# Expert blocks behind run-time branches: order of the two versions, row lists, weight halves, and a version for a last short block

## The chip, the cores and the metric

One core of one Trainium2 chip runs the whole kernel. The metric is the device time of one execution in microseconds (us). The engines are PE (matrix multiplication, with PEld for its weight loads), DVE (vector), ACT (scalar functions), POOL (general purpose; here it issues gathers and scatters) and SP (here it issues plain transfers). Each engine has a sequencer of its own that fetches instructions, waits for semaphores and takes branches; in the profile its rows carry a q (PEldq, DVEq, POOLq).

## The reference, cut to what matters

Three layers in a row, all in float32: local and global attention, a dense layer of width 2048, and a routed layer with 8 experts. The part that the change touches is the last:

```python
skip_score = x @ w_skip
do_compute = skip_score > 0
out = x.copy()
xc = x[do_compute]
logits = xc @ w_gate
e_idx = np.argmax(logits, axis=1)
...
for e in range(E):
    mask = e_idx == e
    if not mask.any():
        continue
    h = np.maximum(xc[mask] @ w1[e], 0.0)
    y[mask] = gate_w[mask, None] * (h @ w2[e])
out[do_compute] = xc + y
```

Which rows go to which expert is known only at run time. For the inputs that are timed, worked out from the reference, 1389 of the 2304 rows are computed: 1116 by expert 3, 241 by expert 0, 32 by expert 5, and none by the other five.

## The kernel before, in words

Attention and the dense layer come first and are not touched. While the dense layer runs, each row tile is routed (`route`, L458): its rows' numbers go to a table in memory, one stretch for each expert, and `choose_first` (L566) picks the expert with most rows so far. Its weights are loaded, split into a high and a low part on ACT and DVE (`split`, L631), and its first 256 rows are computed in code without branches (L804 to L820, the **first block**).

`choose_order` (L581) then sorts what is left: 1116 - 256 = 860 rows of the first expert (called expert 0 from here on, by its place in the order), 241 of expert 1, 32 of expert 2, none of experts 3 to 7. DVE does this with some twenty operations on a single partition, and writes the counts and the start of each row list to `regs` and `nxt`. Each engine loads the 8 counts into registers (L821) and from there on branches on them by itself.

A **block** is `(k, t)`: expert k, its t-th 256 rows. Each block exists in two versions (`products`, L824). The wide one does up to 256 rows: 8 x 12 matmuls to the hidden layer (`mm1`), 8 transposes for the next block's rows, 2 x 8 x 3 matmuls back (`mm2`). The few-row one does up to 128 with the operands exchanged: 24 matmuls of 512 columns (`mm1_few`), 8 transposes of the hidden layer, 24 matmuls back, and 8 transposes for the next block. With these counts the path is (0,0) wide, (0,1) wide, (0,2) wide, (0,3) few (92 rows), (1,0) wide, (2,0) few, and the end.

How the code lies in memory, and so what a branch skips:

- In `block` (L875) the wide version comes first, and the few-row version behind it as `Else`; a wide block ends with a jump past the few-row code.
- In `expert` (L894) the first block of an expert is there twice, with and without loading the next expert's weights (the test on the next count, L896), one behind the other.
- `others` (L888) holds the further blocks of the expert, each inside the test of the one before (L890); an expert that is done jumps past all blocks that it doesn't use (five for expert 0 behind (0,3), five for expert 1, three for expert 2).
- The next expert is inside the test of its count (L904). The end of the kernel lies behind all experts and behind a second copy of them (L909, used when the first expert has nothing left).

Where such paths meet again, every engine brings its semaphores to the same counts: the engine that comes along the shorter path adds what is missing, and first waits until its own work has reached its count. For POOL's semaphores of transfers that means a wait for the landing of its transfers.

What a block does around its matmuls: at its head DVE copies the row list (`cid`), POOL loads the list of the next block (`load_ids`, L877), and DVE and POOL finish the second half of the **block before** (`finish_rows(1)`, `send_rows(1)`, L881: scale, add, scatter to the output). Then the version's own code: POOL gathers the next block's rows (`load_rows`, two gathers of 128 rows), and in an expert's first block SP loads the next expert's weights, chunks 0 and 1 at the head and 2 to 7 behind the gathers; a POOL memset ahead of each group holds SP back until the buffer is free (`prefetch`, L797). The last `finish_rows(1)` and `send_rows(1)` stand behind all branches (L915).

Of the kernel before, what the change touches and what calls it, by code (L numbers as in the profile page):

```python
# [7 lines left out]
F32 = mybir.dt.float32  # L8
# [6 lines left out]
ALU = mybir.AluOpType  # L15
AX = mybir.AxisListType
ET = mybir.EngineType
# [11 lines left out]
NF = FF // 128  # L29
# [18 lines left out]
def tile_kernel(ctx, tc, q, k, v, w_in, w_out, wsg, w1, w2,  # L48
# [532 lines left out]
    def choose_order():  # L581
        cnt = counts()
        nc.vector.scalar_tensor_tensor(out=key, in0=cnt, scalar=8.0, in1=sev[0:1, :], op0=ALU.mult, op1=ALU.add)
        nc.vector.scalar_tensor_tensor(out=key, in0=ohs, scalar=65536.0, in1=key, op0=ALU.mult, op1=ALU.add)
        nc.vector.max(out=top, in_=key)
        nc.vector.tensor_copy(out=ki[:, 0:8], in_=top)
        nc.vector.tensor_scalar(out=regs[:, 8:16], in0=ki[:, 0:8], scalar1=7, scalar2=7, op0=ALU.bitwise_and,
                                op1=ALU.bitwise_xor)
        nc.vector.tensor_scalar(out=ki[:, 8:16], in0=ki[:, 0:8], scalar1=3, scalar2=4095,
                                op0=ALU.arith_shift_right, op1=ALU.bitwise_and)  # L590
        nc.vector.tensor_copy(out=cf, in_=ki[:, 8:16])
        nc.vector.tensor_tensor(out=cf[:, 0:1], in0=cf[:, 0:1], in1=s0, op=ALU.subtract)
# [5 lines left out]
        n1 = mp.tile([1, NE, NBM], F32, name="n1")  # L598
        n2 = mp.tile([1, NE, NBM], F32, name="n2")
        n3 = mp.tile([1, 8], F32, name="n3")  # L600
# [12 lines left out]

    def routing_step(u):
        if rt:
# [208 lines left out]
    def products(k, many, pre):  # L824
        q = k % 2
        todo = [(1 - q, f, raws[f // 2]) for f in range(NF)] if pre else []

        def splits(n=1):
            for _ in range(n):
                if todo:  # L830
                    split(*todo.pop(0))

        if many:
            nc.vector.tensor_copy(out=cyg_, in_=nyg_)
            for f in range(NEF):
                mm1(q, f)
                if f == 1:
                    load_rows()
                    if pre:
                        prefetch(k + 1, range(4 if k == 0 else 2, 8))  # L840
                if f >= (0 if k == 0 else 5):
                    splits()
            nc.vector.tensor_copy(out=pid, in_=cid[:, :, 0:2])
            for s_ in range(2):
                transpose_rows(s_)
            for s_ in range(2):
                for f in range(NEF):
                    mm2(q, s_, s_, f)
                    if f % 2 == 1:
                        splits()  # L850
                if s_ == 0:
                    finish_rows(0)
                    send_rows(0)
        else:
            nc.vector.tensor_copy(out=cyg_[:, 1], in_=nyg_[:, 0])
            load_rows()
            if pre:
                prefetch(k + 1, range(4 if k == 0 else 2, 8))
            mm1_few(q, 0)
            splits(1 if k == 0 else 0)  # L860
# [4 lines left out]
            splits()  # L865
            for f in range(NEF):
                mm2(q, 0, 1, f)
                if f == 1:
                    transpose_few(1)
                if f in (2, 3):  # L870
                    transpose_rows(f - 2)
                splits(2 if f % 2 == 0 else 1)
        splits(NF)

    def block(k, t, pre):  # L875
        nc.vector.tensor_copy(out=cid, in_=nid)
        load_ids(nc.values_load(nxt[0:1, k * NBM + t:k * NBM + t + 1], engines=[ET.Pool], min_val=0,  # L877
                                max_val=NE * CAP))
        if pre and k > 0:
            prefetch(k + 1, range(2))  # L880
        finish_rows(1)  # L881
        send_rows(1)
        with tc.If(cnts[k] > BLK * t + 128) as wide:
            products(k, True, pre)
        with wide.Else():
            products(k, False, pre)

    def others(k, t):  # L888
        if t < NBLK[k]:
            with tc.If(cnts[k] > BLK * t):  # L890
                block(k, t, False)
                others(k, t + 1)

    def expert(k):  # L894
        if k + 1 < NE:
            with tc.If(cnts[k + 1] > 0) as more:  # L896
                block(k, 0, True)
            with more.Else():
                block(k, 0, False)
        else:  # L900
            block(k, 0, False)
        others(k, 1)
        if k + 1 < NE:
            with tc.If(cnts[k + 1] > 0):  # L904
                expert(k + 1)

    with tc.If(cnts[0] > 0) as some:
        expert(0)
    with some.Else():  # L909
        with tc.If(cnts[1] > 0):  # L910
            prefetch(1, range(4, 8))
            for f in range(NF):
                split(1, f, raws[f // 2])
            expert(1)
    finish_rows(1)  # L915
    send_rows(1)


# [102 lines left out]
```

## Time and profile before

| what | us |
|---|---|
| median of 3 runs | 719.22 (717.91 to 720.38) |
| the profiled execution | 719.69 |
| its span, first to last instruction | 717.6 |
| PE busy in the span | 678.9 (95%) |
| mean granted PE clock | 0.984 |

The profiled execution is 0.47 above the median; its span leaves out 2.1 us around the first and last instruction. On the page, PE's row of busy tenths reads 9 or nearly in all but the first and the last slices of the span, and the last two slices read 4 and 3. The chain of work that ended last is PE for 71%, transfers for 8%, and "issue" for 6%: time in which an engine waited for nothing that the profile shows.

### The profile page before, as it was taken

To read this page: it belongs to the slowest core of one execution; us is meant where nothing else is said; L and a number is where in the kernel's file an instruction comes from. 1 tells how busy PE (TensorE), PEld (TensorE's weight loads), DVE (VectorE), ACT (ScalarE), POOL (GpSimd) and SP (SyncE) were. 2 spreads that over 40 slices of the span, in tenths; PEclk is the share of its full clock that TensorE was granted. 3 is DMA by queue.
4 is the path that set the end of the run, shared out by engine and by line. 5 is a ranking of instruction groups with operands and counts; after the bars stand their busy time and mean duration, and the time that the engine had idled before them with its cause. 6 is when DMAs were issued, how large, how long until landed. Compare 5 with 4: busy or idle time off the path is not lost.

```text
span 717.6 us, 11768 instructions
## 1 busy us (share of the span) xinstructions
PE 678.9 (95%) x4081; PEld 562.0 (78%) x4081; DVE 411.9 (57%) x1419; ACT 382.7 (53%) x904; POOL 80.7 (11%) x134
## 2 busy tenths in 40 slices
PE   6999999999999999999999999999999899999843
PEld 4777777778888777788777888898889799988632
DVE  6899999978998333334433254435666483223711
ACT  4888888967997443344433354436663162112501
POOL 2111111100000001000010000020002322222020
PEclk9999999999999999999999999999999999999967
DMA  9656566335540300003000033213101441205520
GB/s 301 187 169 183 169 169 209 117 103 172 158 138 0 118 0 1 1 1 117 1 1 1 1 117 118 59 31 102 47 2 60 157 170 58 60 33 136 195 48 15
DMA packets 28242, 66.83 MB, mean 93 GB/s; under 512 B 3755, under 2 KB 12589, under 8 KB 27108
## 3 DMA queue, kind: packets, MB, share of 16 engines
q1 hardware_dynamic: 25092, 58.41, 25.1%
q0 software_dynamic: 3040, 7.10, 3.6%
q8 instruction: 51, 0.84, 0.6%
q14 instruction: 59, 0.48, 0.3%
HBM read 53.38 MB, written 12.43 MB: 92 GB/s over the span
## 4 chain that ended last, share of the span: by engine, by line
PE 71%; DMA 8%; issue 6%; DVE 5%; ACT 1%; POOL 1%; POOLq 0%; DVEq 0%
PE y L534 26%; PE h L158 26%; DMA nyg<-ys,nid 6%; PE e L664 5%; PE z L699 3%; PE o L305 3%; PE t L290 2%; PE s L252 2%; DMA out_dram<-ob,pid 2%; PE r L465 1%; DVE P_a L261 1%; ACT P_a L268 1%; DVE P_a L284 1%; PE r L469 1%; DMA nid<-table 1%
## 5 line engine op out<-in xcount | busy, mean ns | idle before, releaser
L534 PE MATMUL y<-wout,gh 128*128 128x512 f32 x544 | 139.9, 396 | 0.1
L158 PE MATMUL h<-xh,winH 128*128 128x512 f32 (+2 forms) x320 | 118.2, 369 | 0.0
L534 PEld LDWEIGHTS y<-wout,gh 128*128 128x128 f32 x544 | 99.0, 188 | 20.4 <-issue 1.2
L158 PE MATMUL h<-xh,winL 128*128 128x512 f32 (+2 forms) x320 | 114.6, 358 | 0.0
L158 PE MATMUL h<-xl,winH 128*128 128x512 f32 (+2 forms) x320 | 114.4, 357 | 0.0
L517 DVE SCALAR_TENSOR_TENSOR tb<-tb,h 128x512 f32<-128x512 f32 (+2 forms) x80 | 48.5, 607 | 105.4 <-ACT tb L514 104.8
L513 ACT ACTIVATE tb<-h,misc 128x512 f32<-128x512 f32 (+2 forms) x80 | 49.6, 620 | 78.9 <-PE h L158 66.3
L534 PE MATMUL y<-wout,gl 128*128 128x512 f32 x272 | 74.9, 390 | 0.0
L521 DVE TENSOR_TENSOR gl<-tb,gh 128x512 fp32r<-128x512 f32 (+2 forms) x80 | 48.9, 611 | 41.9 <-ACT gh L518 41.6
L518 ACT ACTIVATE gh<-tb 128x512 fp32r<-128x512 f32 (+2 forms) x80 | 45.4, 567 | 45.0 <-DVE tb L517 44.4
L158 PEld LDWEIGHTS h<-xh,winH 128*128 128x128 f32 x320 | 60.2, 188 | 10.6 <-issue 2.5
L158 PEld LDWEIGHTS h<-xh,winL 128*128 128x128 f32 x320 | 60.2, 188 | 7.8
L158 PEld LDWEIGHTS h<-xl,winH 128*128 128x128 f32 x320 | 60.3, 189 | 7.4
L268 ACT ACTIVATE P_a<-P_a,st 128x160 f32<-128x160 f32 x128 | 53.8, 423 | 15.3 <-DVE st L261 14.4
L500 POOL DMA_INDIRECT table<-ids,slot x17 | 17.3, 1020 | 387.5 <-DVE slot L498 274.1
L534 PEld LDWEIGHTS y<-wout,gl 128*128 128x128 f32 x272 | 51.1, 188 | 11.0
L699 PE MATMUL z<-WA,h 128*128 128x512 f32 x240 | 57.9, 394 | 0.0
L305 PE MATMUL o<-PT,V 128*64 128x160 f32 x512 | 48.9, 311 | 2.6 <-issue 1.4
L699 PEld LDWEIGHTS z<-WA,h 128*128 128x128 f32 x240 | 44.2, 188 | 8.7
L664 PE MATMUL e<-yTH,WA 128*128 128x256 f32 x256 | 48.7, 286 | 0.1
L252 PE MATMUL s<-K,Q 128*128 128x160 f32 x256 | 46.3, 305 | 1.5 <-DVE st L261 1.3
L514 ACT ACTIVATE tb<-tb 128x512 f32<-128x512 f32 (+2 forms) x80 | 45.5, 568 | 2.5
(200 smaller groups left out, 1104.9 us busy)
## 6 DMA issues: line engine op xcount, KB each, us to landing
xr<-in_w_dram SPq DMA_DIRECT2D x24, 512.0 KB, 6.5
V<-in_v_dram SPq DMA_DIRECT2D x8, 1024.0 KB, 5.3
K<-in_k_dram SPq DMA_DIRECT2D x7, 800.0 KB, 5.3
raw<-in_w_in_dram SPq DMA_DIRECT2D x10, 512.0 KB, 6.3
sp<-in_w_out_dram SPq DMA_DIRECT2D x10, 512.0 KB, 4.5
ys<-xT SPq DMA_DIRECT2D x15, 256.0 KB, 3.0
out_dram<-xT SPq DMA_DIRECT2D x15, 256.0 KB, 4.6
Q<-in_q_dram SPq DMA_DIRECT2D x14, 256.0 KB, 6.6
```

Source lines behind the costliest of these rows:

```text
L158: nc.tensor.matmul(hp, lhsT=lw, rhs=rx[:, 0:n], start=(c == 0 and k == 0), stop=(c == 3 and k == 2))
L252: nc.tensor.matmul(s_ps[s % 2][:, a, 0:W], lhsT=Q_b[n % 2][:, i, j, :, :, a].rearrange("p h c -> p (h c)"), rhs=K_b[n % 2][:, i, W * j + 9 ...
L268: nc.scalar.activation(out=px(s, a), in_=px(s, a), func=AF.Exp, bias=st[:, a:a + 1], scale=-1.0, accum_out=st[:, 2 + a:3 + a])
L305: nc.tensor.matmul(o[64 * h:64 * h + 64, 0:W], lhsT=V[:, j, t, i * 128 + h * 64:i * 128 + h * 64 + 64], rhs=PT[:, t, h, :], start=(t == 0) ...
L513: nc.scalar.activation(out=t, in_=hp, func=AF.Relu, bias=half, scale=0.5)
L514: nc.scalar.activation(out=t, in_=t, func=AF.Square)
L517: nc.vector.scalar_tensor_tensor(out=t, in0=t, scalar=1.0, in1=hp, op0=ALU.min, op1=ALU.max)
L518: nc.scalar.activation(out=a, in_=t, func=AF.Copy)
L521: nc.vector.tensor_tensor(out=b_, in0=t, in1=a.bitcast(F32), op=ALU.subtract)
L534: nc.tensor.matmul(y_ps[q], lhsT=(gL if lows else gH)[:, s], rhs=wo(hl, f), start=(f == 0 and hl == 0 and not lows), stop=(f == NF - 1 and ...
L664: nc.tensor.matmul(hp, lhsT=lw, rhs=ry[:, c], start=(n == 0), stop=(n == 11))
L699: nc.tensor.matmul(z_ps[z], lhsT=lh[:, d], rhs=rw, start=(f == 0 and k == 0), stop=(f == NEF - 1 and k == 2))
```

## The change

1. `choose_order` computes, for each block, where the list of the block after next begins (`fr` holds the next ones, `nxt` becomes those one further), and `last[k]`: zero when expert k has at most 128 rows and no expert follows. The 8 values go to `regs[24:32]`, and every engine loads them as a second set of registers (`more`).
2. Row lists are a block further ahead: `next_ids` at the **end** of a block copies `nid` to `cid` and loads the list for the block after next; a block's gathers come at its very start. `finish_rows(1)` and `send_rows(1)` move from the next block's head to the end of the block itself, before its branch.
3. Weights come in two halves: `prefetch(k + 2, range(4))` behind the splits of block (k, 0), and `prefetch(k + 1, range(4, 8))` at the start of block (k, 0). An expert's first block always has the splits of the next expert's weights; they are no longer there in two copies.
4. The few-row version comes first in the code, the wide one behind it as `Else`, and the test for the expert's next block is inside the wide version. Block (1,0) has the wide version alone.
5. Experts 2 to 7 begin with a test of `more[k]`; where it is zero, `last_few` does the one short block with no gathers, no row lists and no transposes for a next block, and with its own finish and send.

```diff
+        last = sc[:, 56:64]
+        nc.vector.tensor_scalar(out=last, in0=cf, scalar1=-128.0, scalar2=0.0, op0=ALU.add, op1=ALU.max)
+        nc.vector.tensor_tensor(out=last[:, 0:7], in0=last[:, 0:7], in1=cf[:, 1:8], op=ALU.max)
+        nc.vector.tensor_copy(out=regs[:, 24:32], in_=last)
...
+        nc.vector.memset(o, float(NE * CAP))
         nc.vector.tensor_scalar(out=n3[:, 0:1], in0=cf[:, 0:1], scalar1=0.0, scalar2=None, op0=ALU.is_gt)
...
-        nc.vector.tensor_tensor(out=n1, in0=n1, in1=n2, op=ALU.mult)
-        nc.vector.tensor_tensor(out=nxt.rearrange("p (k t) -> p k t", k=NE), in0=n1, in1=bk1, op=ALU.add)
+        nc.vector.tensor_tensor(out=n2, in0=n1, in1=n2, op=ALU.mult)
+        nc.vector.tensor_tensor(out=fr[:, 0:NE, 0:NBM], in0=n2, in1=bk1, op=ALU.add)
...
+        nc.vector.tensor_tensor(out=nxt.rearrange("p (k t) -> p k t", k=NE), in0=n2, in1=fk1, op=ALU.add)
...
+    def next_ids(addr):
+        nc.vector.tensor_copy(out=cid, in_=nid)
+        load_ids(addr)
...
-        if q == 0:
-            finish_rows(0)
-            send_rows(0)
+        if q == 1:
+            next_ids(nc.values_load(regs[0:1, 17:18], engines=[ET.Pool], min_val=0, max_val=NE * CAP))
+        finish_rows(q)
+        send_rows(q)
     _, cnts = nc.values_load_multi_w_load_instructions(regs[0:1, 0:NE], min_val=0, max_val=TOK)
+    _, more = nc.values_load_multi_w_load_instructions(regs[0:1, 24:24 + NE], min_val=0, max_val=TOK)
...
+    def products(k, t, many):
         q = k % 2
+        pre = t == 0 and k + 1 < NE
...
         if many:
             nc.vector.tensor_copy(out=cyg_, in_=nyg_)
+            load_rows()
+            if pre:
+                prefetch(k + 1, range(4, 8))
             for f in range(NEF):
                 mm1(q, f)
-                if f == 1:
-                    load_rows()
-                    if pre:
-                        prefetch(k + 1, range(4 if k == 0 else 2, 8))
-                if f >= (0 if k == 0 else 5):
-                    splits()
+                splits()
...
-                if s_ == 0:
-                    finish_rows(0)
-                    send_rows(0)
+                if s_ == 1:
+                    next_ids(after(k, t))
+                finish_rows(s_)
+                send_rows(s_)
         else:
...
+            next_ids(after(k, t))
+            finish_rows(1)
+            send_rows(1)
         splits(NF)
+        if pre and k + 2 < NE:
+            prefetch(k + 2, range(4))
+
+    def last_few(k):
+        q = k % 2
+        nc.vector.tensor_copy(out=cyg_[:, 1], in_=nyg_[:, 0])
+        mm1_few(q, 0)
+        mm1_few(q, 1, range(2))
+        transpose_few(0)
+        mm1_few(q, 1, range(2, 4))
+        nc.vector.tensor_copy(out=pid[:, 1], in_=cid[:, 0, 0:2])
+        for f in range(NEF):
+            mm2(q, 0, 1, f)
+            if f == 1:
+                transpose_few(1)
         finish_rows(1)
         send_rows(1)
...
+    def wide(k, t):
+        products(k, t, True)
+        if t + 1 < NBLK[k]:
+            with tc.If(cnts[k] > BLK * (t + 1)):
+                block(k, t + 1)
+
+    def block(k, t):
+        if (k, t) == (1, 0):
+            wide(k, t)
+            return
+        with tc.If(cnts[k] <= BLK * t + 128) as few:
+            products(k, t, False)
+        with few.Else():
+            wide(k, t)
+
+    def following(k):
+        block(k, 0)
         if k + 1 < NE:
             with tc.If(cnts[k + 1] > 0):
                 expert(k + 1)
+
+    def expert(k):
+        if k < 2:
+            following(k)
+            return
+        with tc.If(more[k] == 0) as end:
+            last_few(k)
+        with end.Else():
+            following(k)
...
-    finish_rows(1)
-    send_rows(1)
```

## Rows read from the trace of the kernel before

**Rows 1.** The page: the span, and one of the queues that bring code.

```profile
span 717.6 us, 11768 instructions
...
q14 instruction: 59, 0.48, 0.3%
```

**Rows 2.** Time line of PE, 565 to 718: start, length, what, and idle time before it.

```profile
569.01 0.66 PE L653 MATMUL p<-ident,nyg 128*128 128x128 f32 x4 [1.06 <-DMA nyg<-ys,nid]
...
641.03 0.39 PE L679 MATMUL e<-WA,yTH 128*128 128x512 f32 x1
...
654.89 0.36 PE L664 MATMUL e<-yTH,WB 128*128 128x256 f32 x1 [0.94 <-DVE ob L704]
...
691.47 0.77 PE L679 MATMUL e<-WA,yTH 128*128 128x512 f32 x1 [13.03 <-issue]
...
704.17 1.75 PE L699 MATMUL z<-WA,h 128*128 128x512 f32 x7
```

**Rows 3.** PE's sequencer between blocks (1,0) and (2,0): branches, ns, start.

```profile
L883 PEldq COMPARE_BRANCH  x1: 3757/3757/3757, 674.2 to 674.2; - x1
...
L890 PEldq COMPARE_BRANCH  x1: 5057/5057/5057, 678.0 to 678.0; - x1
...
L896 PEldq COMPARE_BRANCH  x1: 4629/4629/4629, 683.4 to 683.4; - x1
...
L883 PEldq COMPARE_BRANCH  x1: 3177/3177/3177, 688.1 to 688.1; - x1
```

**Rows 4.** Windows: length, busy time of PE, PEld, DVE, ACT, POOL, then PE's granted clock.

```profile
680.80:691.40 10.60, 0.00 (x0) 0.00 (x0) 1.18 (x2) 0.00 (x0) 3.93 (x4) 0.50 0.33 77
691.40:694.50 3.10, 3.03 (x7) 2.48 (x8) 0.00 (x0) 0.00 (x0) 0.00 (x0) 0.50 0.03 8
```

**Rows 5.** Behind the last matmul: PE's branches, DVE's last operation, the last send.

```profile
L904 PEldq COMPARE_BRANCH  x1: 4993/4993/4993, 706.5 to 706.5; - x1
...
L904 PEldq COMPARE_BRANCH  x1: 4604/4604/4604, 711.7 to 711.7; - x1
...
712.57 0.75 DVE L704 SCALAR_TENSOR_TENSOR ob<-z,pid,cyg 128x512 f32<-128x512 f32 x1 [7.99 <-PEq L904]
...
713.61 1.02 POOL L708 DMA_INDIRECT out_dram<-ob,pid  x1 [25.54 <-DVE ob L704]
```

**Rows 6.** PE's sequencer at two other branches: past the few-row version; out of expert (0).

```profile
L883 PEldq COMPARE_BRANCH  x1: 193/193/193, 613.7 to 613.7; - x1
...
L890 PEldq COMPARE_BRANCH  x1: 3315/3315/3315, 650.5 to 650.5; - x1
```

**Rows 7.** The first block: register load of the counts (PE), one small DVE operation.

```profile
L821 PEldq TENSOR_LOAD <-regs x1: 780/780/780, 569.1 to 569.1; - x1
...
L604 DVE TENSOR_TENSOR regs<-n,sc 1x1 int32<-1x1 f32 x1 | 0.1, 147 | 0.0
```

**Rows 8.** DVE's sequencer at a branch past unused blocks, and its first step behind it, twice.

```profile
L890 DVEq COMPARE_BRANCH  x2: 47/55/63, 651.9 to 652.8; - x2
L890 DVEq EVENT_SEMAPHORE  x1: 21/21/21, 652.7 to 652.7; - x1
...
L890 DVEq COMPARE_BRANCH  x1: 62/62/62, 675.6 to 675.6; - x1
L890 DVEq EVENT_SEMAPHORE  x1: 21/21/21, 679.2 to 679.2; - x1
```

**Rows 9.** POOL at an expert's end: waits for transfers, counts; time behind a far branch.

```profile
L890 POOLq EVENT_SEMAPHORE  x5: 17/43/3889, 644.9 to 649.1; - x5
L890 POOLq INC_SWDGE_SEM  x1: 388/388/388, 649.2 to 649.2; - x1
...
695.96 2.46 issue
```

**Rows 10.** Row gathers issued in 576 to 579, and in 657 to 659: us to landing.

```profile
nyg<-ys,nid POOLq DMA_INDIRECT x2, 3.3
...
nyg<-ys,nid POOLq DMA_INDIRECT x2, 6.1
```

More of the change, by code (lines that the diff above doesn't have):

```diff
@@ L596, in choose_order @@
         nc.vector.tensor_tensor(out=bf[:, 0:1], in0=bf[:, 0:1], in1=s0, op=ALU.add)
-        n1 = mp.tile([1, NE, NBM], F32, name="n1")
-        n2 = mp.tile([1, NE, NBM], F32, name="n2")
-        n3 = mp.tile([1, 8], F32, name="n3")
+        last = sc[:, 56:64]
+        nc.vector.tensor_scalar(out=last, in0=cf, scalar1=-128.0, scalar2=0.0, op0=ALU.add, op1=ALU.max)
+        nc.vector.tensor_tensor(out=last[:, 0:7], in0=last[:, 0:7], in1=cf[:, 1:8], op=ALU.max)
+        nc.vector.tensor_copy(out=regs[:, 24:32], in_=last)
+        o = mp.tile([1, 512], F32, tag="gl0", name="order")
+        n1, n2 = (o[:, 96 * i:96 * i + NE * NBM].rearrange("p (k t) -> p k t", k=NE) for i in range(2))
+        fr = o[:, 192:192 + (NE + 1) * (NBM + 1)].rearrange("p (k t) -> p k t", k=NE + 1)
+        n3 = o[:, 304:312]
+        nc.vector.memset(o, float(NE * CAP))
         nc.vector.tensor_scalar(out=n3[:, 0:1], in0=cf[:, 0:1], scalar1=0.0, scalar2=None, op0=ALU.is_gt)
@@ L610, in choose_order @@
         nc.vector.tensor_tensor(out=n2, in0=n2, in1=bk1, op=ALU.subtract)
-        nc.vector.tensor_tensor(out=n1, in0=n1, in1=n2, op=ALU.mult)
-        nc.vector.tensor_tensor(out=nxt.rearrange("p (k t) -> p k t", k=NE), in0=n1, in1=bk1, op=ALU.add)
+        nc.vector.tensor_tensor(out=n2, in0=n1, in1=n2, op=ALU.mult)
+        nc.vector.tensor_tensor(out=fr[:, 0:NE, 0:NBM], in0=n2, in1=bk1, op=ALU.add)
+        nc.vector.tensor_tensor(out=n3[:, 3:4], in0=fr[:, 0, 0:1], in1=fr[:, 1, 0:1], op=ALU.subtract)
+        nc.vector.tensor_tensor(out=n3[:, 4:5], in0=n3[:, 0:1], in1=n3[:, 3:4], op=ALU.mult)
+        nc.vector.tensor_tensor(out=regs[:, 17:18], in0=n3[:, 4:5], in1=fr[:, 1, 0:1], op=ALU.add)
+        fk1 = fr[:, 1:NE + 1, 0:1].to_broadcast([1, NE, NBM])
+        nc.vector.tensor_tensor(out=n2, in0=fr[:, 0:NE, 1:NBM + 1], in1=fk1, op=ALU.subtract)
+        nc.vector.tensor_tensor(out=n2, in0=n1, in1=n2, op=ALU.mult)
+        nc.vector.tensor_tensor(out=nxt.rearrange("p (k t) -> p k t", k=NE), in0=n2, in1=fk1, op=ALU.add)
     def routing_step(u):
@@ L817, in tile_kernel @@
                 transpose_rows(f - 4)
-        if q == 0:
-            finish_rows(0)
-            send_rows(0)
+        if q == 1:
+            next_ids(nc.values_load(regs[0:1, 17:18], engines=[ET.Pool], min_val=0, max_val=NE * CAP))
+        finish_rows(q)
+        send_rows(q)
     _, cnts = nc.values_load_multi_w_load_instructions(regs[0:1, 0:NE], min_val=0, max_val=TOK)
-    def products(k, many, pre):
+    _, more = nc.values_load_multi_w_load_instructions(regs[0:1, 24:24 + NE], min_val=0, max_val=TOK)
+    def products(k, t, many):
         q = k % 2
-        todo = [(1 - q, f, raws[f // 2]) for f in range(NF)] if pre else []
+        pre = t == 0 and k + 1 < NE
+        todo = list(range(NF)) if pre else []
         def splits(n=1):
@@ L830, in splits @@
                 if todo:
-                    split(*todo.pop(0))
+                    f = todo.pop(0)
+                    split(1 - q, f, raws[f // 2])
         if many:
             nc.vector.tensor_copy(out=cyg_, in_=nyg_)
+            load_rows()
+            if pre:
+                prefetch(k + 1, range(4, 8))
             for f in range(NEF):
                 mm1(q, f)
-                if f == 1:
-                    load_rows()
-                    if pre:
-                        prefetch(k + 1, range(4 if k == 0 else 2, 8))
-                if f >= (0 if k == 0 else 5):
-                    splits()
+                splits()
             nc.vector.tensor_copy(out=pid, in_=cid[:, :, 0:2])
@@ L857, in products @@
             if pre:
-                prefetch(k + 1, range(4 if k == 0 else 2, 8))
+                prefetch(k + 1, range(4, 8))
             mm1_few(q, 0)
-            splits(1 if k == 0 else 0)
             mm1_few(q, 1, range(2))
@@ L864, in products @@
             nc.vector.tensor_copy(out=pid[:, 1], in_=cid[:, 0, 0:2])
-            splits()
             for f in range(NEF):
@@ L871, in products, with after @@
                     transpose_rows(f - 2)
-                splits(2 if f % 2 == 0 else 1)
+                splits()
+            next_ids(after(k, t))
+            finish_rows(1)
+            send_rows(1)
         splits(NF)
[L875 to L880, printed above, removed]
+        if pre and k + 2 < NE:
[12 more added lines that the diff above has]
+                transpose_few(1)
         finish_rows(1)
         send_rows(1)
[L883 to L902, printed above, removed]
+    def after(k, t):
+        return nc.values_load(nxt[0:1, k * NBM + t:k * NBM + t + 1], engines=[ET.Pool], min_val=0, max_val=NE * CAP)
+    def wide(k, t):
[13 more added lines that the diff above has]
+        block(k, 0)
         if k + 1 < NE:
@@ L913, in tile_kernel @@
                 split(1, f, raws[f // 2])
+            prefetch(2, range(4))
             expert(1)
-    finish_rows(1)
-    send_rows(1)
 def _constants():
```

## The prediction

> **What bounds the kernel now.** The page first: in a span of 717.6 [rows 1] PE is busy almost everywhere and the chain is mostly PE's own, so the span changes with PE's work and with the time in which PE stands. Then PE's time line from the first block on, read for its idle times [rows 2]: four blocks of the first expert follow each other without a gap, (0,3) to (1,0) has 0.94 us, and (1,0) to (2,0) has 13.03, put down to "issue": no data was missing. The sequencer's rows say what it was [rows 3]: four taken branches of 3.76 + 5.06 + 4.63 + 3.18 = 16.6 us. The first began at 674.2, 4.2 ahead of PE's last matmul (691.47 - 13.03 = 678.44), because the sequencer runs ahead of the array; so 12.4 of them lie in the open, and 0.6 of small steps make up the 13.03. [...] Block (2,0) took 704.17 + 1.75 - 691.47 = 14.45, the same code in (0,3) 654.89 - 0.94 - 641.03 = 12.92. Third, the end [rows 5]: the last matmul ends at 705.92, two more far branches take PE 4.99 and 4.60, and DVE's last `finish_rows(1)`, behind all branches, starts at 712.57 only, because PE brings its semaphore up to the count behind the first of them. From the last matmul to the end of the span are 717.6 - 705.92 = 11.7 us. So 26 of the last 40 us are no work.
>
> Not every branch costs this [rows 6]: a wide block's jump past the few-row code takes 0.19, and the jump out of expert 0 takes 3.3, nearly all of it under matmuls still queued.
>
> **The change, step by step,** against the profiled 719.69 (span 717.6), which stands 0.47 above the median of 719.22. A difference under 0.3%, 2.2 us, can't be told from none.
>
> *First block, +1.3.* Ten more small DVE operations in `choose_order`. Four come ahead of `regs[16]`: three of 0.15 [rows 7] and the clearing of 512 numbers, not seen in the trace; about 0.6 in sum. POOL's list load, the two gathers and PE's transposes hang on it, and PE already waits 1.06 there for the gather [rows 2], so the 0.6 goes through. The other six lie beside that same wait. Then PE loads a second set of counts: 0.78 [rows 7], with PE's queue as good as empty at that point, since its sequencer has just been held by the gather. The new branch into the wide version skips the few-row code: 0.2 as in [rows 6], of which I count nothing separately. SP, POOL, ACT and DVE load the set too; POOL's row list and gathers for the next block lie 12 us ahead of their use, and chunks 4 to 7 are asked for earlier than before. Sum 1.4, taken as 1.3; bounds 0 (all under other waits) and +2.5.
>
> *(0,0) to (0,3): 0.* Each now ends with its own list load, finish and send instead of the next head having them: the same instructions in nearly the same order on DVE and POOL; PE's jump is the 0.19 kind. The transfer of chunks 0 to 3 of expert 2 moves under (0,1), where nothing waits for it. If its traffic slows a gather from 3.3 to 6.1 [rows 10], that is still half a block early.
>
> *(0,3) to (1,0), +0.3.* PE's far jump (past (0,3) wide and five further blocks) is alone, as the 3.3 of [rows 6], and begins 3.4 ahead of the last matmul, so PE starts about 0.5 behind it (an estimate: the 0.94 without the filling up of counts). But DVE now waits for the last matmul with `finish_rows(1)` **before** its own far jump. A far jump takes DVE 0.8 or 3.6 [rows 8], I take 2.7, near POOL's 2.5 behind a single one [rows 9]. It then copies `cyg` and takes the first hidden tile off its accumulator, two operations of the size of the 0.75 in [rows 5] or less: that is done 4.2 after the last matmul. PE has two accumulators. A wide block's 23.55 (678.44 - 654.89) hold 96 matmuls of 256 columns and 48 of twice as many, so a tile's 12 take 1.47; PE needs the accumulator at 0.5 + 2.9 = 3.4 and waits 0.8. Net 0.5 + 0.8 - 0.94 = +0.3. POOL is worse off: its send must land before it leaves the block, as it waited 3.89 for its gathers [rows 9]; then 0.4 for the counts and 2.5 for the jump. With 4.1 to the landing (1.05 to the send's start as in [rows 5], and about 3 from there), the gathers start at 7.3 and 8.7 behind the last matmul and land 3.3 later [rows 10], the second at 12.0; PE needs them at 12.5 to 13. No cost, but no cover either: at 6.1 [rows 10] PE would wait 2. Chunks 4 to 7 are asked for at about 10, with 14 us of the block left for their landing and splits; before, six of the eight were asked for behind the gathers of this same block. Bounds -0.7 and +2.5.
>
> *(1,0) to (2,0), -11.0.* Three of the four branches go: no few-row code behind (1,0), no second copy, and the last version lies directly behind its test. What stays is the jump past expert 1's five unused blocks: alone, 3.3 to 3.8, begun 4.2 early, hidden. Then PE fills up its count and passes two tests: 0.9 as in the 0.94 of [rows 2]. In its way stands DVE again: PE's first matmul needs a count that DVE reaches only behind its own jump, and DVE jumps after its finish. (Before, DVE was through at 652.7, ahead of PE's last matmul at 653.95 [rows 2, 8], so no row prices this.) With 0.8 or 2.7 for that, PE stands 1.0 or 2.9; I take 2.0, the middle, as the rows hold both. 13.03 - 2.0 = 11.0. Bounds -12.1 and -8.5.
>
> *(2,0) itself, -2.3.* No half clock: 14.45 to 12.92. Without the 8 transposes of a next block 12.2: 0.7 for two fours, which overlap their neighbours, 0.66 each at most [rows 2]. The weights are there: all splits are done in (1,0). If PE stands as long as 2.4, the clock may fall as in [rows 4]; then 0.8 is left of the gain.
>
> *The end, -3.8.* `finish_rows(1)` starts at the last matmul, the send 1.05 later (713.61 - 712.57 in [rows 5]), and from a send's start to the end of the span took 717.6 - 713.61 = 4.0. But POOL now has branches **behind** the send: it waits for its landing, fills up its counts, 0.4, and jumps past all experts, 2.5 [rows 9]. 1.05 + 4.0 + 0.4 + 2.5 = 7.9 against 11.7. PE's and DVE's far jumps, 5.0 at most, end before that. Bounds -6 (jump under the landing) and 0 (two jumps, each with waits).
>
> Sum: 1.3 + 0.3 - 11.0 - 2.3 - 3.8 = -15.5; 719.69 - 15.5 = 704.2, on the median 703.7.
>
> How far a jump must go to cost something, the rows don't say, only that both kinds occur. One of the two queues that bring code moves 0.48 MB in 59 packets, 8 KB each [rows 1]. [...]
>
> **Rivals.**
>
> A, the forecast: 703.7, chance 0.63.
>
> B, DVE's code is always there: both DVE jumps take 0.8. PE stands 1.0 at (2,0) and starts (1,0) 0.4 earlier: 1.0 + 0.7 less, 702.0. For it the 0.8 at 651.9, against it the 3.6 at 675.6 [rows 8], though that came right behind another jump. Chance 0.15.
>
> C, the end gains nothing: POOL needs two jumps and two rounds of waits behind the send. 3.8 more, 707.5. For it: before, POOL went through two such rounds at the end, each with its 2.5; against it: behind `last_few` there is nothing left to test. Chance 0.13.
>
> D, slower: the code to be skipped, now in front. At the heads of (0,0), (0,1), (0,2) and behind (0,3) PE takes a jump; if each were of the far kind and in the open, as those of [rows 3], at 5.06 each they cost 20.2, and the time is 703.7 + 20.2 = 723.9. It turns slower than before by over 2.2 from 17.7 in sum, 4.4 each. Against it: 0.19 for the same distance [rows 6], and a sequencer that is 4 us ahead at each block's end. Chance 0.04.
>
> E, the change doesn't do what it says for these counts: `more[2]` isn't zero and (2,0) takes the ordinary few-row version. Then the transposes and tests come back and the end has a second jump: 0.7 + 3.8 more, 708.2. The counts, 32 and none behind, speak against it. Chance 0.03; 0.02 is left for no difference at all.
>
> **The numbers.** The likeliest is A, 703.7. The range goes down to 700.5 (B, with the first block's steps hidden) and up to 708.0 (C, or A with a late gather and a fallen clock). Faster by over 2.2: A, B, C and E less a little, 0.93; same 0.03; slower 0.04, D.
>
> **What would show it.** PE idle ahead of (2,0) of 1 to 3 with a single far branch in that stretch; the clock at 1.0 through (2,0); DVE's last finish within 0.2 of the last matmul; a POOL far branch as the last thing before the end. A gap over 4 at (2,0), or one of over 1 within expert 0's wide blocks, or an end of over 10, proves that step wrong.

## The result, and the profile after

The changed kernel takes 709.03 us (median of 4 runs, 707.35 to 710.52), the kernel before 719.8 in the runs beside it (4 runs, 717.91 to 721.87): a ratio of 0.9849, 95% interval 0.9813 to 0.9885, so 1.5% faster. Forecast were 703.7 and a range of 700.5 to 708.0. The sign was right; the size was 11 us instead of 16, and the time lies outside the range.

The profiled execution took 710.52, span 708.8, against 717.6 [rows 1]. It is the slowest of the four, 1.5 above their median, so its stages come to less than the 10.8 between the medians. By stages, each from one last matmul to the next first or last one:

| stage | before | after | difference | forecast |
|---|---|---|---|---|
| to the last matmul of (0,3) | 653.95 | 655.83 | +1.9 | +1.3 |
| from there to the last matmul of (1,0) | 24.49 | 29.53 | **+5.0** | +0.3 |
| PE idle ahead of (2,0) | 13.03 | 3.23 | -9.8 | -11.0 |
| (2,0) itself | 14.45 | 13.69 | -0.8 | -2.3 |
| last matmul to the end | 11.7 | 6.5 | -5.2 | -3.8 |
| sum (the two spans; rows rounded) | 717.6 | 708.8 | -8.8 | -15.5 |

Four steps are right or off by about 1.5; one is wrong by 4.7. PE's time line of the changed kernel (start, length, what, and in brackets the idle time before it with what ended it) shows where, next to [rows 2]:

```profile
656.12 0.35 PE L678 MATMUL e<-yTH,WB 128*128 128x256 f32 x1 [0.29 <-issue]
659.47 0.58 PE L678 MATMUL e<-yTL,WB 128*128 128x256 f32 x1 [2.99 <-issue]
...
688.60 0.47 PE L693 MATMUL e<-WA,yTH 128*128 128x512 f32 x1 [3.23 <-DVEq L922]
```

PE starts (1,0) 0.29 behind (0,3), earlier than the 0.94 of before. Then it does one matmul and stands for 2.99 us. The windows (length, busy time of PE, PEld, DVE, ACT, POOL, then the granted clock, as in [rows 4]) show what follows; the first is the stretch in the kernel before, the others are the changed kernel:

```profile
653.95:678.44 24.49, 23.55 (x152) 21.32 (x152) 16.00 (x29) 12.35 (x26) 5.66 (x7) 1.00 0.66 217
...
655.83:685.36 29.53, 26.25 (x152) 23.82 (x152) 17.28 (x31) 12.35 (x26) 5.67 (x6) 0.88 0.36 109
...
658.22:665.04 6.82, 5.57 (x26) 5.58 (x27) 1.81 (x3) 1.16 (x3) 2.67 (x3) 0.50 0.24 67
...
688.93:692.35 3.42, 3.42 (x10) 2.68 (x9) 0.43 (x1) 0.00 (x0) 0.00 (x0) 0.50 0.03 7
```

The granted clock fell from 1.00 to 0.50 while PE stood, and 5.6 us of the block's first matmuls ran at about half their rate: 26 of them took 5.57 us at 0.50 (third line), the 26 behind them, from 665.04 to 668.00, took 2.96 at 1.00. Of the stretch's 5.0, 2.7 are PE's longer busy time (26.25 instead of 23.55) and 2.3 its longer standing. Ahead of (2,0) PE stood 3.23, the clock fell to 0.50 at 688.93, 0.33 behind the start of its first matmul there, and stayed there for 3.4 us.

At the other places the sequencer's rows look as forecast. One far branch is left on PE at each of the two changes of expert, begun under queued matmuls, against one [rows 6] and four [rows 3]; and the end has one, begun ahead of the last matmul, against two [rows 5]. (Columns: ns, shortest, median and longest, then first and last start in us.)

```profile
L929 PEldq COMPARE_BRANCH  x1: 3419/3419/3419, 652.4 to 652.4; - x1
...
L922 PEldq COMPARE_BRANCH  x1: 3309/3309/3309, 681.1 to 681.1; - x1
L922 PEldq EVENT_SEMAPHORE  x1: 51/51/51, 685.4 to 685.4; - x1
L922 DVEq COMPARE_BRANCH  x1: 63/63/63, 685.4 to 685.4; - x1
...
L922 DVEq EVENT_SEMAPHORE  x1: 21/21/21, 688.4 to 688.4; - x1
...
L944 PEldq COMPARE_BRANCH  x1: 3329/3329/3329, 699.8 to 699.8; - x1
```

The middle rows are the 3.23: PE is through its branch at 684.4 and adds its own count at 685.4, behind its last matmul, but its next matmul needs a count that DVE brings at 688.4 only. DVE began its branch at 685.4, since its finish had waited for the same last matmul; its next step came 3.0 later.

DVE's time line around the two ends of a block holds the row that matters most:

```profile
655.87 0.75 DVE L717 SCALAR_TENSOR_TENSOR ob<-z,pid,cyg 128x512 f32<-128x512 f32 x1 [1.29 <-PE z L713]
660.40 0.69 DVE L857 COPY cyg<-nyg 128x1024 f32<-128x1024 f32 x1 [3.78 <-DMA out_dram<-ob,pid]
...
702.33 0.75 DVE L717 SCALAR_TENSOR_TENSOR ob<-z,pid,cyg 128x512 f32<-128x512 f32 x1 [2.62 <-PE z L713]
```

The last line is the finish at the end: it starts 0.04 behind the last matmul (702.29), where it was 6.7 behind it before (712.57 in [rows 5], last matmul 705.92). The second line says that DVE, after its jump into (1,0), stood 3.78 us for the landing of a **send**, one that it has no use for. The send's own rows, and the steps with which DVE waits ahead of its copy:

```profile
L721 POOL DMA_INDIRECT out_dram<-ob,pid x1: 1023/1023/1023, 656.9 to 656.9; - x1
...
DMA to landing us min/median/max: 3.1/3.1/3.1
...
L857 DVEq EVENT_SEMAPHORE  x4: 49/50/50, 660.0 to 660.3; - x4
...
L929 POOLq COMPARE_BRANCH  x1: 43/43/43, 657.2 to 657.2; - x1
```

The send starts at 656.9 and lands 3.1 later, at 660.0, when DVE's steps begin; POOL took its branch at 657.2, long before the landing. In this kernel DVE's lateness is not seen on PE, because PE's own wait lay over it.

### The profile page after: what moved, and what is told of

It is laid out like the page before. It is cut to its first block, busy times and chain, and to the rows that moved or that the text cites. A ratio compares the mean times of both kernels' runs of the same rounds, so it can differ in the third digit from the quotient of the medians.

```text
span 708.8 us, 11698 instructions
## 1 busy us (share of the span) xinstructions
PE 682.4 (96%) x4073; PEld 563.8 (80%) x4073; DVE 412.2 (58%) x1427; ACT 382.0 (54%) x902; POOL 79.2 (11%) x133
## 5 line engine op out<-in xcount | busy, mean ns | idle before, releaser
L682 ACT ACTIVATE h<-e 128x256 fp32r<-128x256 f32 x40 | 15.3, 383 | 58.7 <-PE e L678 34.2
```

## The experiments

Two things were late at (1,0) at once: PE's code and DVE. My first reading of DVE's 3.78 was a far jump, as at 685.4; so the first theories were a "code theory" (PE's 2.99 alone is the loss) and a "DVE theory" (its jump is). The stretch in all tables is the one from the last matmul of (0,3) to that of (1,0): 24.49 before, 29.53 after.

### Two causes, taken away one by one and together

**e1_place** moves PE's code only:

```
             nc.vector.tensor_copy(out=pid, in_=cid[:, :, 0:2])
+            if (k, t) == (0, 7):
+                for _ in range(34):
+                    nc.tensor.transpose(p_ps[0][:, 0, :], nyg_[:, 0, 0:128], ident)
```

> The changed kernel with 34 transposes more in the wide version of block (0,7), which never runs: nothing is executed that was not before, only PE's code behind it lies 68 instructions further on. In the changed kernel PE's first packet of code for (1,0) is asked for at 653.36 and a second at 656.57, and PE stands 2.99 us after one matmul of (1,0), just until behind the second. Code theory: (1,0) begins at the very end of a piece of code, the next piece is asked for only when the first is entered, and that alone is the loss. Then the 2.99 goes, the clock stays at 1.0, and from the last matmul of (0,3) to that of (1,0) takes 24.5 to 25 instead of 29.5; time 704 to 705. DVE theory: DVE comes out of its own far jump 4.2 us after the last matmul, so the third hidden tile has no accumulator. Then PE runs two tiles (2.9 us), stands 2 to 3 us there instead, the clock falls all the same, and the stretch takes 27.5 to 29.5; time 707 to 709.

**e2_defer** moves the last finish and send only (shown is the few-row version; the wide one and the first block lose their second finish and send in the same way, `last_few` has the two lines at its head too, and the paths with no further expert get them in an Else):

```
     def products(k, t, many):
...
+        finish_rows(1)
+        send_rows(1)
         if many:
...
             next_ids(after(k, t))
-            finish_rows(1)
-            send_rows(1)
         splits(NF)
```

> The changed kernel with finish_rows(1) and send_rows(1) of a block again at the head of the next one (as in the kernel before), last_few keeping its own. PE's code lies where it did. DVE now jumps without waiting for the last matmul. Code theory for (1,0): PE still stands 2.5 to 3 us after its first matmul and the clock falls, 28.5 to 29.5 for the stretch. DVE theory for (1,0): the stretch falls to 24.5 to 25.5. Both say of (1,0) to (2,0): PE's first matmul no longer waits for DVE's jump, the gap falls from 3.23 to 0.9 to 1.3 and (2,0) from 13.7 to about 12.2, since the clock does not fall there: 3.5 less. If the gap stays above 2.5, DVE's jump was not what PE waited for. Time 705 to 706 by the code theory, 700 to 702 by the DVE theory.

**e3_both** has both edits.

> Both edits: PE's code 68 instructions further on, and the last finish and send of a block at the head of the next. If each of the two lateness (PE's second piece of code, DVE's jump) is enough to hold PE for some 3 us at (1,0), only this kernel gets the 5 us back: the stretch 24.3 to 25, no half clock after 650, gap ahead of (2,0) 0.9 to 1.3, time 699.5 to 702. If one of them alone was the cause, this run equals the one of the first two that removes it, plus 3.5 for (2,0) if that is the first.

| kernel | time (median) | ratio to before, 95% | stretch | PE stands in (1,0) | ahead of (2,0) | (2,0) |
|---|---|---|---|---|---|---|
| after | 709.03 | 0.9813 to 0.9885 | 29.53 | 2.99 after 1 matmul | 3.23 | 13.7 |
| e1_place | 707.5 | 0.9789 to 0.9854 | 26.30 | 1.98 after 24 | 3.09 | 14.9 |
| e2_defer | 704.5 | 0.9757 to 0.9809 | 28.63 | 2.94 after 1 | 0.55 | 12.1 |
| e3_both | 700.53 | 0.9713 to 0.9745 | 25.05 | 0.78 after 24 | 0.55 | 12.1 |

PE's time line in e1_place:

```profile
656.08 0.35 PE L678 MATMUL e<-yTH,WB 128*128 128x256 f32 x1 [0.52 <-issue]
...
661.16 0.39 PE L678 MATMUL e<-yTH,WB 128*128 128x256 f32 x1 [1.98 <-DVE h L683]
```

in e2_defer:

```profile
659.32 0.39 PE L678 MATMUL e<-yTL,WB 128*128 128x256 f32 x1 [2.94 <-issue]
...
684.83 0.47 PE L693 MATMUL e<-WA,yTH 128*128 128x512 f32 x1 [0.55 <-PEq L926]
```

and in e3_both:

```profile
659.00 0.39 PE L678 MATMUL e<-yTH,WB 128*128 128x256 f32 x1 [0.78 <-DVE h L683]
```

With the code moved, PE no longer stands behind its first matmul, and nothing that runs was changed: so the 2.99 was code that was not there. It then meets the next late thing, DVE's first hidden tile (L683), two tiles of 12 matmuls on, as the DVE theory has it. With finish and send moved instead, the 2.94 stays and the gap ahead of (2,0) closes, to 0.55 where 0.9 to 1.3 was expected. Only both together give most of the 5 us back; 0.78 is left. Neither theory alone was right: the code alone would have given 24.5 to 25 in e1_place, DVE alone 24.5 to 25.5 in e2_defer. The DVE theory missed in e1_place as well (27.5 to 29.5, with a fallen clock): PE stood about as long as it says, but the clock did not fall in (1,0) (1.00 over the 26.30). By time alone e1_place can't be told from the changed kernel, as their intervals overlap; its stretch is read from the trace.

### How far from the next piece of code

**e7_place15** is e3_both with `range(115)` in place of `range(34)`.

> As e3_both, but with 115 dead transposes instead of 34, which puts the first matmul of (1,0) some 28 instructions, 14 matmuls, ahead of the place at which PE's next piece of code begins (after a single matmul in e2_defer, after some 95 in e3_both). Code theory: the second piece is asked for when the jump ends and is there 3.4 us later, as in e2_defer; 14 matmuls of 0.107 cover 1.5 of it, so PE stands 1.6 to 2.1 there and nowhere else in (1,0) before: stretch 25.6 to 26.3 at full clock, time 701 to 702. If the place of the code did not matter, (1,0) would look as in e3_both: 0.8 behind 24 matmuls, 25.05.

PE's time line:

```profile
659.48 0.50 PE L678 MATMUL e<-yTH,WB 128*128 128x256 f32 x2 [1.73 <-issue]
...
661.39 0.58 PE L678 MATMUL e<-yTH,WB 128*128 128x256 f32 x1 [0.46 <-DVE h L683]
```

It stands 1.73 (1.6 to 2.1 expected), after 14 matmuls (14 expected). The "some 95" of the expectation for e3_both stays an estimate (14 and the 115 - 34 = 81 transposes between the two kernels): there PE stands only once in (1,0), 0.78 behind 24 matmuls, and that for DVE. So the place in the code decides, and how much: what the matmuls ahead of the border cover is saved. PE goes on 3.35 behind the start of its first matmul of (1,0) in the changed kernel, 3.30 in e2_defer and 3.63 here, whether one matmul or 14 lie ahead of the border; 14 take 1.7 in these rows, not the 1.5 reckoned. The stretch missed: 27.92, because DVE was late as well (0.46) and the granted clock fell (0.94 in the mean of the stretch, as 3.4 us at 0.50 would give; from 661.77 on single matmuls take 0.41 instead of 0.28, until 664.31); time 702.49 (ratio 0.9721 to 0.9762).

PE's code comes in packets of 16 KB: the queue q8 moves 0.67 MB in 41 of them in the changed kernel. (That q8 is PE's is taken from its rate: from 200 to 400 us it moves 7 packets while PE takes 1910 instructions, 273 for each.) In the changed kernel's transfers by queue (packets, MB, share of the window), the window 653.2 to 654.6 holds one, under PE's branch (3.42 from 652.4 on); the window 656.4 to 658.2 holds the next, which moved only after PE had entered the block at 656.1; and none lies between:

```profile
q8 instruction: 1, 0.02, 5.0%
...
q8 instruction: 1, 0.02, 5.2%
```

### No far jump at all

**e4_nblk1** writes out one block for expert 1, **e8_near** also four for expert 0:

```
-NBLK = [9, 6, 4, 3, 2, 2, 2, 2]
+NBLK = [9, 1, 4, 3, 2, 2, 2, 2]
...
+NBLK = [4, 1, 4, 3, 2, 2, 2, 2]
```

> The changed kernel with one block instead of six written out for expert 1 (enough for these counts, not in general): nothing is skipped between (1,0) and (2,0), so neither PE nor DVE jumps far there; finish and send stay where the change put them. Up to (1,0) nothing differs, 5 us late again. DVE theory for the gap ahead of (2,0): DVE needs no new code behind its finish, gap 3.23 to 0.5 to 1.2, (2,0) 13.7 to 12.2 at full clock; time 3.5 to 4.5 less, about 705. If the gap came from something else, from the tests or the filling up of counts, it stays above 2.

> The changed kernel with four blocks written out for expert 0 and one for expert 1 (enough for these counts, not in general): no engine jumps far before the end; finish and send stay where the change put them. If finish_rows(1) ahead of the jump is bad only because a far jump follows, PE now stands 0.3 to 0.6 ahead of (1,0) and under 0.5 in it, the stretch takes 24 to 24.6, the gap ahead of (2,0) is 0.3 to 0.6 with no half clock before the end: 703.3 - 4.5 = 698 to 699.5, under e3_both. If finish_rows(1) at the block's end costs PE by itself (DVE 1.5 us late with the first hidden tile), the stretch stays above 25.

e4_nblk1: 703.26 (0.9744 to 0.9797). PE passes from (1,0) to (2,0) without a gap (0.5 to 1.2 expected), at full clock, and (2,0) takes 12.0:

```profile
681.81 1.98 PE L713 MATMUL z<-WB,h 128*128 128x512 f32 x8
683.62 0.39 PE L693 MATMUL e<-WA,yTH 128*128 128x512 f32 x1
```

So DVE's 3.0 ahead of (2,0) was its far jump; e2_defer closed the gap in the other way, by letting DVE jump early. Some 1.7 of the gain is not the edit's, in the two profiled executions: the clock stayed low for 3.4 in (1,0) (0.96 in the mean of 655 to 695.63) instead of 6.8.

e8_near: 701.88 (0.9728 to 0.9768), and here the DVE theory fell. PE has its code; but its and DVE's time lines are

```profile
659.22 0.39 PE L678 MATMUL e<-yTH,WB 128*128 128x256 f32 x1 [2.26 <-DVE h L683]
```

```profile
654.13 0.75 DVE L717 SCALAR_TENSOR_TENSOR ob<-z,pid,cyg 128x512 f32<-128x512 f32 x1 [1.29 <-PE z L713]
658.14 0.69 DVE L857 COPY cyg<-nyg 128x1024 f32<-128x1024 f32 x1 [3.25 <-DMA out_dram<-ob,pid]
```

Without any far jump DVE still stands 3.25, again for the landing of the send; PE stands 2.26, the clock falls for 3.4 (single matmuls take 0.41 instead of 0.28 from 660.26 to 662.82), the stretch is 27.3 instead of 24 to 24.6, and the time lies above the 698 to 699.5 expected. The bracket says what the wait is: at the join of the two versions of a block the program makes DVE's first operation wait for POOL's transfers (the four steps of L857 above, which begin at 660.0, with the landing), and the send is the last of them. In the kernel before the four steps stood there too (L876, 50 ns each, 653.1 to 653.4), but list load and send were issued **behind** the join, at the next block's head, so nothing was under way. DVE's first operation there waited only for its own branch, and the list load that hangs on it began at 654.18:

```profile
653.50 0.17 DVE L876 COPY cid<-nid 128x8 int32<-128x8 int32 x1 [0.89 <-DVEq L890]
```

### The landing

In e2_defer the send is behind the join, but the row list is loaded just ahead of it, and DVE's time line there names that:

```profile
659.45 0.75 DVE L717 SCALAR_TENSOR_TENSOR ob<-z,pid,cyg 128x512 f32<-128x512 f32 x1 [5.06 <-DMA nid<-table]
```

So a third theory, the "landing theory", with two kernels. **e9_list** is e3_both and

```
             nc.vector.tensor_copy(out=pid, in_=cid[:, :, 0:2])
+            next_ids(after(k, t))
...
-                if s_ == 1:
-                    next_ids(after(k, t))
...
             nc.vector.tensor_copy(out=pid[:, 1], in_=cid[:, 0, 0:2])
+            next_ids(after(k, t))
...
-            next_ids(after(k, t))
         splits(NF)
```

> As e3_both, but every block copies its row list and loads the next one right behind its copy of pid, ahead of its second product, instead of at its end. In the seven kernels with the few-row block ahead of (1,0) changed or not, DVE's first instruction there began 0.03 us behind the landing of a transfer that POOL had issued last: the send (after, e1_place, e4_nblk1, e8_near) or, where the send is at the next head, the list load (e2_defer, e3_both, e5_head, e7_place15). Landing theory: at the join of the two versions DVE waits for all of POOL's transfers, and its jump is covered by that. With the list load some 5 us earlier nothing is left to wait for, DVE is ready before PE, PE stands under 0.2 after its first matmul of (1,0) and the stretch takes 23.9 to 24.3 instead of 25.05 (25.7 to 28 in e5_head): time 699.3 to 699.9, and less spread. Jump theory: DVE needs its code until about 3.4 us after its branch at 652.7 anyway, PE still stands 0.5 to 0.8 behind 24 matmuls: 700.3 to 700.7.

**e10_send** has the code's place and the early list too, but leaves `finish_rows(1)` in place and moves only the send to the next head:

```
             finish_rows(1)
-            send_rows(1)
         splits(NF)
...
+        send_rows(1)
         if many:
             nc.vector.tensor_copy(out=cyg_, in_=nyg_)
```

> As e1_place (PE's code 68 instructions further on, finish_rows(1) in place at the block's end, ahead of the jumps), but the block's last send goes to the head of the next block and the row list is loaded early as in e9_list. DVE still jumps only behind the last matmul. Landing theory: DVE no longer waits for the send, its first hidden tile is taken off 2.0 to 2.3 behind the last matmul instead of 5.6, PE stands under 0.4 in (1,0), stretch 24 to 24.6 against 26.30 in e1_place. Jump theory: DVE's code alone takes it 3 to 3.6 as at (1,0) to (2,0) (3.02 there), PE stands 1.5 to 2.2 behind 24 matmuls as in e1_place, stretch 25.8 to 26.4. At (1,0) to (2,0) both leave the gap at 3, since there DVE passed its branch without any transfer to wait for. Time 705 to 706 or 707 to 708.

DVE's time line in e10_send, where it still jumps only behind the last matmul:

```profile
655.27 0.75 DVE L717 SCALAR_TENSOR_TENSOR ob<-z,pid,cyg 128x512 f32<-128x512 f32 x1 [1.37 <-PE z L713]
656.31 0.73 DVE L859 COPY cyg<-nyg 128x1024 f32<-128x1024 f32 x1 [0.28 <-DVE ob L717]
```

and its branch, with the first steps behind it:

```profile
L934 DVEq COMPARE_BRANCH  x1: 53/53/53, 655.3 to 655.3; - x1
...
L859 DVEq EVENT_SEMAPHORE  x4: 49/50/50, 655.9 to 656.2; - x4
```

The copy follows 0.28 behind the finish instead of 3.78. DVE's branch costs about 0.5 here; why the one ahead of (2,0) costs 3.0, the runs do not show. PE does not stand in (1,0) behind its first matmul; stretch 24.14, as the landing theory has it, and the gap ahead of (2,0) stays at 3.10, as both have it. The time, 702.71 (0.9714 to 0.9773), is below the 705 to 706 expected; the clock did not fall behind that gap:

```profile
679.38:682.48 3.10, 0.01 (x2) 0.03 (x1) 0.75 (x1) 0.00 (x0) 0.00 (x0) 1.00 0.05 13
682.48:694.58 12.10, 12.10 (x56) 9.69 (x56) 2.03 (x6) 2.52 (x6) 0.98 (x1) 1.00 0.06 23
```

e9_list, windows (columns as above) of (1,0), the gap, (2,0) and the end:

```profile
655.11:679.01 23.90, 23.54 (x152) 21.31 (x152) 17.44 (x31) 12.35 (x26) 5.41 (x7) 1.00 0.42 133
679.01:679.63 0.62, 0.00 (x1) 0.03 (x1) 0.11 (x1) 0.00 (x0) 0.00 (x0) 1.00 0.18 40
679.63:691.75 12.12, 12.12 (x56) 9.68 (x56) 2.66 (x7) 2.51 (x6) 0.98 (x1) 1.00 0.06 22
691.75:697.80 6.05, 0.00 (x1) 0.00 (x0) 0.75 (x1) 0.00 (x0) 0.98 (x1) 0.85 0.07 19
```

Of the 23.90 only 0.36 is idle, and the 0.78 of e3_both is gone. The time is **699.34** (5 runs, 699.24 to 699.83; ratio 0.9697, interval 0.9669 to 0.9724): 9.7 under the changed kernel (10.9 by the two ratios, as the kernel before was 1.7 slower beside it), with a spread of 0.6 where that has 3.2. It keeps every block, so by its code it serves any counts; it was run with these alone.

### The first block, and the last part alone

**e5_head** is e3_both with the order of work in `choose_order` and the second load of counts changed:

```
+    more = {}
-    _, more = nc.values_load_multi_w_load_instructions(regs[0:1, 24:24 + NE], min_val=0, max_val=TOK)
...
+                    if (k, t, s_, f) == (1, 0, 0, 4):
+                        _, more[0] = nc.values_load_multi_w_load_instructions(regs[0:1, 24:24 + NE], min_val=0, max_val=TOK)
```

> The kernel with both edits (e3_both), and in its first block: regs[16] (which the next row list hangs on) is worked out ahead of the four operations of the change that stood before it, and the second set of counts is loaded by every engine in the middle of (1,0) instead of ahead of (0,0). Theory: both lie on PE's way, 0.5 for the four operations and 0.6 for the load (PE's second load took 0.60 in all runs so far), so PE reaches (0,0) and everything after 0.9 to 1.2 earlier, and the load in (1,0) costs nothing, since 10 matmuls of 0.23 are queued there: 699.3 to 699.8. Rival: PE is held there by the gather's landing, which differs by about 1 us from run to run anyway; then only the 0.6 goes, or nothing can be told: 699.8 to 700.7.

700.64 (0.9707 to 0.9743; 699.57 to 703.82), not to be told from e3_both, and in the rival's range. Its profiled execution is the slowest, 703.82. There PE starts (0,0) at 570.30 instead of 571.14, but then stands in it (PE's time line):

```profile
583.96 0.66 PE L666 MATMUL p<-ident,nyg 128*128 128x128 f32 x4 [1.40 <-DMA nyg<-ys,nid]
```

In e3_both PE goes on there at 583.70, having stood 0.14: in these two traces the gather landed no earlier for the PE that started earlier. So what PE loses at its start need not show at the end of (0,0); with one trace of each this is argued, not shown. What makes this execution slow lies elsewhere: DVE stood 5.40 for the list ahead of (1,0), PE 2.49 for DVE, and the clock fell (0.94 in the mean of the stretch).

**e6_nolast** takes `last_few` away:

```
     def expert(k):
-        if k < 2:
-            following(k)
-            return
-        with tc.If(more[k] == 0) as end:
-            last_few(k)
-        with end.Else():
-            following(k)
+        following(k)
```

> The changed kernel without last_few: (2,0) takes the ordinary few-row version, with its gathers, its row list and 8 transposes, its finish and send still in place. PE's code up to (1,0) lies where it did. If the end's 5.2 (11.7 to 6.5) came from last_few, because two rounds of tests and far jumps are back behind the send, the end takes 9.5 to 11 again and (2,0) 0.7 more: 712.5 to 714. If it came from finish_rows(1) standing ahead of the jumps, the end stays at 6.5 to 7.5: 709.5 to 710.5.

722.63 (ratio 1.0032, interval 1.0016 to 1.0047): without this part the change gains nothing over the kernel before, and it is 13.6 above the changed one (some 13 by the two ratios); I had expected 3.5 to 5, or about nothing. (2,0) grew by 0.9 only, but from the last matmul (701.63) to the end (720.8) are 19.2. DVE's time line there:

```profile
703.55 0.75 DVE L717 SCALAR_TENSOR_TENSOR ob<-z,pid,cyg 128x512 f32<-128x512 f32 x1
704.21 4.90 DVE L649 TENSOR_TENSOR WB<-xr,WB 128x512 fp32r<-128x512 f32 x8
```

DVE splits the weights of an expert that never comes, POOL's last send takes 5.00 beside it, and PE takes two far branches, 4.73 and 5.31, instead of one. The kernel before had a copy of each block without this preparation (`pre`); the change gave that copy up and needs `last_few` in its place.

## Why the prediction was wrong, and where it was right

**First block, +1.3.** Held within its bounds: +1.9 in this trace; in the five traces whose code up to there is the same (after, e1_place, e4_nblk1, e6_nolast, e8_near) (0,3) ends at 655.83, 655.56, 655.44, 655.04 and 654.09, a mean of 1.24 behind the 653.95 of before. The kernel before is a single trace here. PE's second load took 0.60, not 0.78.

**(0,0) to (0,3), 0, and rival D.** The branches at the heads of the wide blocks took 0.35, 0.21 and 0.21 on PE, with a gap of 0.26 at most; D is out, and so is E, since (2,0) took `last_few`.

**(0,3) to (1,0), +0.3: the step that failed,** at +5.0, in two terms. The first is PE's jump: it "is alone", "so PE starts about 0.5 behind it". PE started, 0.29 behind; but one matmul on its code ended, and the next piece came 2.99 later. My bounds knew far branches by the duration of their own row, not by what comes behind them; e1_place and e7_place15 show it. The second term is DVE's. I had it done 4.2 behind the last matmul, 2.7 of that a jump, and PE waiting 0.8 for it. In e1_place, where DVE alone holds PE, PE goes on 5.6 behind (661.16 - 655.56) after standing 1.98; what it waits for is the send's landing, while the jump that I had at 2.7 took about 0.5 in e10_send. In the changed kernel this term lay under the first and cost nothing more; it shows as soon as the first is gone. The prediction did see that wait and put it on the wrong engine: "POOL is worse off: its send must land before it leaves the block". POOL left at 657.2 with the send still under way, and DVE waited. And the fallen clock, which I had priced for (2,0), was not in the bounds of this step: 5.6 us of matmuls at half rate, 2.7 of the 5.0. Without the 4.7 by which this step missed, the time would have been 704.3, near the forecast.

**(1,0) to (2,0), -11.0.** Right in kind: one far branch on PE, hidden; PE's first matmul waiting for the count that DVE brings behind its own jump. That jump took 3.0, the upper value, 2.7, and a little more; so 3.23 instead of 2.0. e2_defer and e4_nblk1 take it away in two ways and both close the gap. Rival B, both DVE jumps at 0.8, is out by this one; for the jump into (1,0) it had the better value, as e10_send shows.

**(2,0), -2.3.** Measured -0.8, which is the case the text named: "If PE stands as long as 2.4, the clock may fall", with 0.8 left of the gain. The 2.4 is one reading: before, the clock was still granted at 1.00 in the 2.36 from PE's last matmul of (1,0) to 680.80, and at 0.50 from there to 694.50 [rows 4]; here it fell after 3.23 of standing and 0.33 of matmuls. At full clock (2,0) took 12.0 to 12.1 in the eight kernels where it did not fall there; the forecast had 12.2.

**The end, -3.8.** Measured -5.2, near the bound of -6: the finish stood 0.04 behind the last matmul, and POOL's count and jump, which I added up behind the send, lay beside its landing. The send began at 703.67 and took 3.4 to land, and the end of the span came 1.7 later. Rival C is out. e6_nolast shows that the price of the part is larger than the step: some 13 lie between having `last_few` and not, since with it go the splits that nobody needs.

## What to carry to other kernels

With the last transfer of a block moved ahead of a join of two code versions, DVE, whose first operation behind the join waits for POOL's transfers, stood for that landing: 3.78 us in the changed kernel, 3.25 in e8_near. With the send behind the join and the list load ahead of the second product it went on after 0.28 (e10_send): put a transfer behind such a join, or well ahead of it. PE's far branch into (1,0) had two prices here: its own row (3.42, under queued matmuls) and, as one matmul later the next packet of code was not there, a second one (2.99); in a row with "[... <-issue]" a few matmuls into a block, look at the packets of code. And where several things are late at one place, taking away one shows only the next: e1_place gave back 3.2 of the stretch's 5.0 and e2_defer 0.9, both together 4.5.

## What the runs showed of the hardware that was not expected

The clock does not follow the length of an idle time in a simple way here. PE stood 2.99 (after) and 2.94 (e2_defer) at the same place, and the clock then stayed low for 6.8 and for 3.4 us; 3.09 (e1_place), 3.23 (after) and 3.10 (e10_send) ahead of (2,0) were followed by 6.8, 3.4 and nothing; 1.98 in (1,0) (e1_place) by nothing, 2.26 at the same place (e8_near) by 3.4. It fell while PE stood in the changed kernel (1.74 after its one matmul had ended) and 0.34 after PE had gone on in e2_defer. Two of these stretches as windows, e1_place behind the 3.09 and e2_defer behind the 2.94:

```profile
684.13:690.96 6.83, 6.01 (x14) 4.83 (x15) 0.43 (x1) 0.37 (x1) 0.18 (x2) 0.50 0.11 39
```

```profile
659.66:663.07 3.41, 3.41 (x19) 3.41 (x18) 1.94 (x4) 0.90 (x2) 2.28 (x2) 0.50 0.17 60
```

What decides between them, the runs do not show; terms for it are therefore bounds, not values.
